# Attention inner loop: weighing in two halves of 256 queries, one ring of seven single PSUM banks, one exponential per head

## The chip, the cores and the metric

The kernel runs on one NeuronCore of a Trainium2 chip. It is written for five engines that each work through their own list of instructions in order: TensorE (PE in the profile, with its weight loads as PEld), VectorE (DVE), ScalarE (ACT), GpSimd (POOL) and SyncE (SP, which issues most DMAs). The metric is the device time of one execution, in microseconds (us); lower is better. All times below are of this one core.

## The reference

One transformer block over 2048 tokens with 576 features: pre-norm attention with 32 heads of 18 features, then a gated GELU network, both with a residual.

```python
# x: [1, 2048, 576]; H = 32, Dh = 18, Df = 4608
def _A_ref(x, wqkv, wo):
    qkv = (x @ wqkv).reshape(B, S, 3, H, Dh).transpose(2, 0, 3, 1, 4)
    q, k, v = qkv[0], qkv[1], qkv[2]
    scores = jnp.einsum("bhqd,bhkd->bhqk", q, k) * Dh ** -0.5
    o = jnp.einsum("bhqk,bhkd->bhqd", softmax(scores), v)
    return o.transpose(0, 2, 1, 3).reshape(B, S, D) @ wo

h  = x + _A_ref(layernorm(x), wqkv, wo)
h2 = h + einsum(gelu(layernorm(h) @ w_gate) * (layernorm(h) @ w_up), w_down)
```

## The kernel before

The program has three stages. The first normalizes the tokens, splits matrices into a high and a low half-precision part, and makes the queries, keys and values. The second is attention, and the change lies there. The third is the gated network.

**Blocks and steps.** The attention loop (L1219) runs over 32 blocks `n` (`NS`), each of one group of four heads and 512 queries. Inside a block it runs over 16 key tiles `kt` of 128 keys. One pass of that inner loop is called a step here, and an even step with the odd one behind it a pair of steps, since the pattern of the work repeats every two. A block is eight pairs.

**What a step does.**

- Scores. `scores_pair` (L667) is called twice. It multiplies 128 keys with 512 queries for two heads into the two halves of a double bank of PSUM (`pair`, two of them, used in turn): two matmuls (L674) of 56 rows each, one on array rows 0 to 55, the other on rows 64 to 119. One ACT instruction (L676) takes the exponential of both halves, 128x1024, into a buffer `pes` in the region `WK`. The double bank is free again when that exponential has ended.
- Maxima. A softmax needs the largest score of each query. `maxima` (L740) computes them a block and a half ahead of the scores. For each pair of steps it makes eight units of 128 queries by 512 keys, each a matmul (L621) of 54 rows into a single bank. Six of them are reduced by DVE to one maximum per query (L633). The other two go together: `over` is passed through a Relu by ACT (L627) into a row buffer, and `both` is added to that row and reduced by a custom DVE instruction (L631). `max_banks` (L611) issues one or two units in one go, and the loop takes five such portions per pair. The single banks are three, used in turn (`m_ring`, the first three of `singles`). At the end of a block's units `max_finish` (L638) reduces the maxima over the keys (L642) and sends them through POOL and two DMAs into the query rows.
- Weighing. `weigh` (L678) multiplies the exponentials of the step before with the values, for four heads, into the accumulator, the fourth of the single banks. Each head has 32 columns of the array (18 values, a one whose sum is the divisor, and padding). The operands are single precision, and the program's four matmuls of 512 queries are eight matmul records in the trace, which run as two batches of four at a time.

When a block's last weighing is done, in the first step of the next block, `out_block` (L688) starts: ACT copies the accumulator into `oT` (L694), a DMA fetches the sums, at `kt` 2 POOL inverts them (a power of -1 over 128x16, L703, and one correction), and at `kt` 4 the result is scaled and written into the transposed input of the output projection.

**What sets the order.** In this stage PE, DVE, ACT and POOL carry out their instructions in the order in which the program text issues them (a manual schedule); semaphores are the only waits. So the order of the calls inside the loop is the order on each engine. An even step before is: a portion of maxima, scores of heads 0 and 1, a portion, scores of heads 2 and 3, other work, a portion, the weighing of the step before. An odd step leaves out the middle portion. The other work (`fill`, `side`) is empty in most blocks; in the last three blocks it holds the output projection of finished queries (`wo_block`) and preparations for the third stage.

Before the loop, the maxima of a block and a half are made beside the remaining products for queries, keys and values (L1216).

Of the kernel before, what the change touches and what calls it, by code (L numbers as in the profile page):

```python
# [12 lines left out]
F32 = mybir.dt.float32  # L13
# [5 lines left out]
P = 128  # L19
# [12 lines left out]
def tile_block(  # L32
# [43 lines left out]
    psp = pairs_in.enter_context(tc.tile_pool(name="psp", bufs=1, space=bass.MemoryType.PSUM))  # L76
    pairs2 = [psp.tile([P, 2, 512], F32, name=f"pair{i}") for i in range(2)]

# [3 lines left out]

    pair_ring = ring(pairs2)
    m_ring = ring(singles)
# [274 lines left out]
    def v_rows(t):  # L359
        for i in range(2):  # L360
            pt = next(pair_ring)[:, 0]
# [61 lines left out]
    def idle_products(n):  # L423

        for _ in range(n):
            nc.tensor.matmul(pairs2[0][:, 0], id16, parts[0][:, :512], start=True, stop=True)

    def turned(t0):

        cols = slice(t0 * P, (t0 + 2) * P)  # L430
        pts = [pairs2[0][:, 1], pairs2[1][:, 0], next(m_ring), next(m_ring)]
# [12 lines left out]
        nc.scalar.copy(XT[:, NK, cols], pt[:, : 2 * P])  # L444
# [165 lines left out]

    def max_banks(n, mx, todo):  # L611

        g, qc = divmod(n, NB)
        pms = []
        for kind, t, kc, h in todo:
            Q, K = sets[g % 2][h // 2]
            q0 = qc * TB + t * P
            r = half(h % 2, R1)
            pm = next(m_ring)
            keys = steps[g % 2][r, kc // 2] if kind == "over" else K[r, kc * TB : (kc + 1) * TB]  # L620
            nc.tensor.matmul(pm[:, :TB], Q[r, q0 : q0 + P], keys, start=True, stop=True)  # L621
            pms.append(pm)
        for (kind, t, kc, h), pm in zip(todo, pms):
            dst = mx[:, t, h, kc : kc + 1]
            if kind == "over":
                row = next(rows_of)
                nc.scalar.activation(row, pm[:, :TB], AF.Relu)  # L627
                excess.append(row)
            elif kind == "both":
                row = excess.pop(0)  # L630
                nc.vector.tensor_tensor_reduce(row, pm[:, :TB], row, 1.0, LOWEST, ALU.add, ALU.max, dst)  # L631
            else:
                nc.vector.tensor_reduce(dst, pm[:, :TB], axis=AX.X, op=ALU.max)  # L633

# [31 lines left out]

    def scores_pair(n, kt, pr):  # L667

        g, qc = divmod(n, NB)
        pS = next(pair_ring)  # L670
        Q, K = sets[g % 2][pr]
        for j in range(2):
            r = half(j, R1 + 2)
            nc.tensor.matmul(pS[:, j, :TB], K[r, kt * P : (kt + 1) * P],  # L674
                             Q[r, qc * TB : (qc + 1) * TB], start=True, stop=True)
        nc.scalar.activation(pes[(2 * kt + pr) % NPE], pS[:, :, :TB], AF.Exp, scale=ex_reg)  # L676

    def weigh(n, kt, acc):  # L678
        for hh in range(4):
            nc.tensor.matmul(acc[32 * hh : 32 * hh + 32, :TB],  # L680
                             Vg[n // NB][:, kt * G4 + hh * VC : kt * G4 + hh * VC + 32],
                             pes[(2 * kt + hh // 2) % NPE][:, hh % 2],
                             start=(kt == 0), stop=(kt == NT - 1))

# [3 lines left out]
    def out_block(n, acc):  # L688
# [4 lines left out]
        oT = oTs[n % 2]  # L693
        nc.scalar.copy(oT, acc[:, :TB])  # L694
        R = 4 * TB // P
# [4 lines left out]
        if n < NS - NB:  # L700
            den, rc = rc, small.tile([P, R], F32, tag="rp", name="rp")
            re = small.tile([P, R], F32, tag="re", name="re")
            nc.gpsimd.tensor_tensor(rc, den, minus_one.to_broadcast([P, R]), op=ALU.pow)  # L703
            nc.gpsimd.tensor_mul(re, den, rc)
# [37 lines left out]
    def maxima():  # L742

        for n in range(NS):
# [449 lines left out]
    def other_products():  # L1194
        for b in range(1, NB):
            yield from v_block(b)
        for j in (1, 6, 2, 7, 3, 8):
            for b in range(1, NB):
                yield from qk_tile(j, b, next(pair_ring)[:, 0])

# [15 lines left out]
    for i in range(5 * AHEAD // 4):  # L1216
        take(mxs, 2)
# [53 lines left out]
    run(side)  # L1271
    weigh(*prev)
    ob = out_block(prev[0], prev[2])
# [102 lines left out]
```

## Time and profile before

| | us |
|---|---|
| median of 3 runs | 2652.98 (2652.97 to 2656.34) |
| the profiled execution | 2654.51 |
| its span in the trace | 2652.7 |
| attention loop in that span, first exponential to last | 216.6 to 1417.7 |

The span is the stretch from the first to the last instruction in the trace; the execution's time is 1.8 us longer. In the loop the granted clock of TensorE is 1.00. The whole profile is one execution. Its page gives busy time by engine and by source line; the timeline gives instructions in order of time, with neighbours of one kind merged (x2 is two of them, and the time is from the first one's start to the last one's end). An engine starts its next instruction before the one before has ended, so the distance from start to start is less than the duration. A PE record shows when a matmul was dispatched; two matmuls on different rows of the array run at the same time.

Busy shares in two stretches, from the windows view:

```profile
1284.80:1332.80 48.00, 46.35 (x333) 16.18 (x325) 42.03 (x90) 34.94 (x42) 32.01 (x43) 1.00 0.15 38
1381.20:1417.70 36.50, 33.27 (x242) 9.36 (x239) 29.23 (x64) 31.76 (x35) 28.55 (x43) 1.00 0.66 97
```

The columns are the stretch, its length, the busy time (and number of instructions) of PE, PEld, DVE, ACT and POOL, the granted clock, the share of the DMA engines that is busy and the GB/s that they move. The first is block 29, with projection products beside the attention; the second is block 31, the last, in which no maxima are left to make.

### The profile page before, as it was taken

To read this page: it belongs to the slowest core of one execution; us is meant where nothing else is said; L and a number is where in the kernel's file an instruction comes from. 1 tells how busy PE (TensorE), PEld (TensorE's weight loads), DVE (VectorE), ACT (ScalarE), POOL (GpSimd) and SP (SyncE) were. 2 spreads that over 40 slices of the span, in tenths; PEclk is the share of its full clock that TensorE was granted. 3 is DMA by queue.
4 is the path that set the end of the run, shared out by engine and by line. 5 is a ranking of instruction groups with operands and counts; after the bars stand their busy time and mean duration, and the time that the engine had idled before them with its cause. 6 is when DMAs were issued, how large, how long until landed. Compare 5 with 4: busy or idle time off the path is not lost.

```text
span 2652.7 us, 44543 instructions
## 1 busy us (share of the span) xinstructions
PE 2585.1 (97%) x16669; PEld 1118.4 (42%) x16669; DVE 2012.4 (76%) x3856; ACT 1621.0 (61%) x2128; POOL 788.2 (30%) x1076
## 2 busy tenths in 40 slices
PE   7999999999999999999999999999999999999999
PEld 4542222222222222222234555555555555555555
DVE  7368999999999999999967766666666666666653
ACT  5227999999999999999865433333333333333332
POOL 4200442221323232322666432222222222222221
PEclk9999999999999999999999999999999999999999
DMA  7411210010101010100116311010101010111110
GB/s 215 97 49 39 56 42 18 27 31 19 43 15 41 15 43 19 40 17 19 39 51 130 73 42 38 25 38 27 36 27 36 27 36 28 35 29 34 30 58 36
DMA packets 169099, 114.11 MB, mean 43 GB/s; under 512 B 88504, under 2 KB 147404, under 8 KB 168882
## 3 DMA queue, kind: packets, MB, share of 16 engines
q1 hardware_dynamic: 161198, 98.47, 13.9%
q0 software_dynamic: 7552, 12.79, 1.9%
q8 instruction: 130, 2.13, 0.3%
q14 instruction: 87, 0.71, 0.1%
q10 hardware_dynamic: 132, 0.01, 0.0%
HBM read 76.51 MB, written 15.01 MB: 35 GB/s over the span
## 4 chain that ended last, share of the span: by engine, by line
PE 68%; ACT 16%; issue 8%; DVE 4%; DMA 2%; POOL 2%; SPq 1%; ACTq 0%; DVEq 0%; POOLq 0%
PE more L1097 14%; PE bank L1097 14%; PE bank L300 11%; ACT WK L676 11%; PE bank L680 9%; PE more L300 8%; PE bank L621 7%; ACT nat L627 4%; PE pair L300 4%; PE pair L674 2%; DVE mx L633 1%; DMA nat<-rc 1%; DVE st L188 0%; DMA V<-V 0%; ACT nat L694 0%
## 5 line engine op out<-in xcount | busy, mean ns | idle before, releaser
L676 ACT ACTIVATE WK<-pair 128x1024 f32<-128x1024 f32 x1024 | 1000.0, 1041 | 83.4 <-PE pair L674 83.1
L633 DVE TENSOR_REDUCE mx<-bank 128x1 f32<-128x512 f32 x1552 | 975.7, 683 | 44.3 <-PE bank L621 33.6
L680 PE MATMUL bank<-WK,V 128*32 128x512 f32 x4096 | 547.1, 605 | 0.2 <-ACT nat L694 0.2
L300 PEld LDWEIGHTS <-WK 128*128 128x128 f16 x3456 | 338.8, 98 | 91.8 <-ACT WK L1108 1.7
L1097 PEld LDWEIGHTS <-W 128*128 128x128 f16 x2394 | 234.0, 98 | 283.2 <-issue 5.5
L621 PE MATMUL bank<-W 54*128 54x512 f16 x896 | 258.1, 379 | 14.5 <-DVE mx L633 2.2
L621 PE MATMUL bank<-A 54*128 54x512 f16 x904 | 250.9, 380 | 19.2 <-DMA nat<-qk_hi 3.2
L703 POOL TENSOR_TENSOR rp<-rc,minus_one 128x16 f32<-128x16 f32 x28 | 81.9, 2927 | 540.2 <-DMA rc<-nat 540.2
L300 PE MATMUL more<-W,WK 128*128 128x288 f16 x1728 | 235.9, 286 | 2.2 <-ACT WK L1108 1.4
L300 PE MATMUL bank<-W,WK 128*128 128x288 f16 x1728 | 236.7, 287 | 0.0
L1097 PE MATMUL bank<-X,W 128*128 128x512 f16 x792 | 223.8, 379 | 0.0
L674 PE MATMUL pair<-W 56*128 56x512 f16 x1024 | 210.0, 380 | 4.1 <-ACT WK L676 3.1
L674 PE MATMUL pair<-A 56*128 56x512 f16 x1024 | 212.1, 380 | 0.5 <-DMA A<-mT 0.3
L1097 PE MATMUL bank<-V,W 128*128 128x512 f16 x720 | 202.4, 379 | 0.4 <-ACT tmp L1147 0.3
L968 POOL TENSOR_TENSOR A<-A 128x384 f32<-128x384 f32 x136 | 137.1, 1029 | 200.4 <-DMA A<-in_B_w_up_dram 101.3
L621 PEld LDWEIGHTS <-W 54*128 54x128 f16 x1024 | 75.1, 93 | 284.2 <-issue 266.3
L631 DVE CUSTOM_DVE_ANT_0 nat<-bank,nat 128x512 f32<-128x512 f32 x248 | 171.4, 691 | 25.4 <-PE pair L674 2.4
L621 PEld LDWEIGHTS <-A 54*128 54x128 f16 x1024 | 71.6, 93 | 272.1 <-issue 250.8
L1111 POOL TENSOR_TENSOR WK<-tmp,WK 128x512 f16<-128x512 f32 x73 | 87.9, 1203 | 308.4 <-ACT WK L1108 308.3
L1115 ACT COPY tmp<-more 128x512 f32<-128x512 f32 x36 | 21.0, 583 | 239.1 <-PE more L1097 198.9
L627 ACT ACTIVATE nat<-bank 128x512 f32<-128x512 f32 x248 | 151.5, 611 | 14.7 <-PE bank L621 14.7
L680 PEld LDWEIGHTS bank<-WK,V 128*32 128x32 f32 x4096 | 81.1, 108 | 178.2 <-issue 163.4
(312 smaller groups left out, 3270.8 us busy)
## 6 DMA issues: line engine op xcount, KB each, us to landing
A<-in_B_w_down_dram SPq DMA_DIRECT2D x8, 1152.0 KB
nat<-rc SPq DMA_DIRECT2D x32, 256.0 KB
A<-in_B_w_gate_dram SPq DMA_DIRECT2D x64, 128.0 KB
A<-in_B_w_up_dram SPq DMA_DIRECT2D x64, 128.0 KB
qk_hi<-tmp SPq DMA_DIRECT2D x36, 128.0 KB
qk_lo<-tmp SPq DMA_DIRECT2D x36, 128.0 KB
out_dram<-nat SPq DMA_DIRECT2D x16, 288.0 KB
X<-nat SPq DMA_DIRECT2D x100, 36.0 KB
```

The source lines that it names most:

```text
L300: nc.tensor.matmul(dst, a, b, start=(i == 0), stop=(i == len(pairs) - 1))
L621: nc.tensor.matmul(pm[:, :TB], Q[r, q0 : q0 + P], keys, start=True, stop=True)
L627: nc.scalar.activation(row, pm[:, :TB], AF.Relu)
L631: nc.vector.tensor_tensor_reduce(row, pm[:, :TB], row, 1.0, LOWEST, ALU.add, ALU.max, dst)
L633: nc.vector.tensor_reduce(dst, pm[:, :TB], axis=AX.X, op=ALU.max)
L674: nc.tensor.matmul(pS[:, j, :TB], K[r, kt * P : (kt + 1) * P], Q[r, qc * TB : (qc + 1) * TB], start=True, stop=True)
L676: nc.scalar.activation(pes[(2 * kt + pr) % NPE], pS[:, :, :TB], AF.Exp, scale=ex_reg)
L680: nc.tensor.matmul(acc[32 * hh : 32 * hh + 32, :TB], Vg[n // NB][:, kt * G4 + hh * VC : kt * G4 + hh * VC + 32], pes[(2 * kt + hh // 2) % ...
L703: nc.gpsimd.tensor_tensor(rc, den, minus_one.to_broadcast([P, R]), op=ALU.pow)
L968: op(W8[:, d], W8[:, a], W8[:, b])
L1097: nc.tensor.matmul(bank, w, x_, start=start and i == 0, stop=i == len(mm) - 1, skip_group_check=not start)
L1111: nc.gpsimd.tensor_sub(hl[:, 2 * i + j], v, hh[:, 2 * i + j])
```

## The change

In words:

- The two double banks become four single ones, and in the loop all seven banks beside the accumulator are one ring, `m_ring`, out of which scores and maxima take their banks one after the other as the program issues them.
- `scores_pair` becomes `score`: one head, one matmul, one exponential over 128x512.
- `max_banks` becomes `max_bank`: one unit at a time. The order of the eight units of a pair is slightly different.
- `weigh` is a generator of two halves of 256 queries. Each half has its own four matmuls.
- The order inside a step is written as a string: `s` one head's scores, `m` one unit of maxima, `w` one half of the weighing, `f` the other work. It is `ssmsmmfwmsw` in an even step and `mssmssmfwwm` in an odd one.
- The copy of the accumulator (L694) goes to DVE, except in the last two blocks.
- POOL's power of -1 over 128x16 becomes four over 128x4, and the later parts of `out_block` come at `kt` 3 and 5 in place of 2 and 4.
- In the first stage the products use the four new single banks in turn where they used the first half of each of two double banks.

```diff
-    pairs2 = [psp.tile([P, 2, 512], F32, name=f"pair{i}") for i in range(2)]
+    quads = [psp.tile([P, 512], F32, name=f"quad{i}") for i in range(4)]
...
-    def scores_pair(n, kt, pr):
+    def score(n, kt, hh):
 
         g, qc = divmod(n, NB)
-        pS = next(pair_ring)
-        Q, K = sets[g % 2][pr]
-        for j in range(2):
-            r = half(j, R1 + 2)
-            nc.tensor.matmul(pS[:, j, :TB], K[r, kt * P : (kt + 1) * P],
-                             Q[r, qc * TB : (qc + 1) * TB], start=True, stop=True)
-        nc.scalar.activation(pes[(2 * kt + pr) % NPE], pS[:, :, :TB], AF.Exp, scale=ex_reg)
+        pS = next(m_ring)
+        Q, K = sets[g % 2][hh // 2]
+        r = half(hh % 2, R1 + 2)
+        nc.tensor.matmul(pS[:, :TB], K[r, kt * P : (kt + 1) * P],
+                         Q[r, qc * TB : (qc + 1) * TB], start=True, stop=True)
+        nc.scalar.activation(pes[(2 * kt + hh // 2) % NPE][:, hh % 2], pS[:, :TB], AF.Exp, scale=ex_reg)
 
     def weigh(n, kt, acc):
-        for hh in range(4):
-            nc.tensor.matmul(acc[32 * hh : 32 * hh + 32, :TB],
-                             Vg[n // NB][:, kt * G4 + hh * VC : kt * G4 + hh * VC + 32],
-                             pes[(2 * kt + hh // 2) % NPE][:, hh % 2],
-                             start=(kt == 0), stop=(kt == NT - 1))
+        for q in range(2):
+            qs = slice(q * TB // 2, (q + 1) * TB // 2)
+            for hh in range(4):
+                nc.tensor.matmul(acc[32 * hh : 32 * hh + 32, qs],
+                                 Vg[n // NB][:, kt * G4 + hh * VC : kt * G4 + hh * VC + 32],
+                                 pes[(2 * kt + hh // 2) % NPE][:, hh % 2, qs],
+                                 start=(kt == 0 and q == 0), stop=(kt == NT - 1 and q == 1))
+            yield
...
-        nc.scalar.copy(oT, acc[:, :TB])
+        (nc.scalar.copy if n >= NS - 2 else nc.vector.tensor_copy)(oT, acc[:, :TB])
...
-            nc.gpsimd.tensor_tensor(rc, den, minus_one.to_broadcast([P, R]), op=ALU.pow)
+            for c in range(0, R, 4):
+                nc.gpsimd.tensor_tensor(rc[:, c : c + 4], den[:, c : c + 4],
+                                        minus_one.to_broadcast([P, 4]), op=ALU.pow)
...
-                for todo in (((over, t, k + 1, 0), ("one", t, k, 1)),
-                             (("one", t, k + 1, 1),),
-                             (("one", t, k, 2), ("one", t, k, 3)),
-                             ((both, t, k, 0),),
-                             (("one", t, k + 1, 2), ("one", t, k + 1, 3))):
-                    max_banks(n, mx, todo)
+                for unit in (("one", t, k, 1), (over, t, k + 1, 0), ("one", t, k + 1, 1), ("one", t, k, 2),
+                             ("one", t, k, 3), (both, t, k, 0), ("one", t, k + 1, 2), ("one", t, k + 1, 3)):
+                    max_bank(n, mx, *unit)
                     yield
...
-    m_ring = ring(singles[:3])
+    m_ring = ring(singles[:3] + quads)
+    STEPS = ("ssmsmmfwmsw", "mssmssmfwwm")
...
-            take(mxs)
-            scores_pair(n, kt, 0)
-            if kt % 2 == 0:
-                take(mxs)
-            scores_pair(n, kt, 1)
-            if n < NS - 1 or kt < 11:
-                take(fill, 2)
-            take(side)
-            take(mxs)
-            if prev is not None:
-                weigh(*prev)
-                if prev[0] != n:
-                    ob = out_block(prev[0], prev[2])
-                    next(ob)
+            heads = iter(range(4))
+            halves = weigh(*prev) if prev is not None else iter(())
+            for step_no, step in enumerate(STEPS[kt % 2]):
+                if step == "s":
+                    score(n, kt, next(heads))
+                elif step == "m":
+                    take(mxs)
+                elif step == "w":
+                    take(halves)
+                    if kt == 0 and step_no == OUT_AT and prev is not None:
+                        ob = out_block(prev[0], prev[2])
+                        next(ob)
+                else:
+                    if n < NS - 1 or kt < 11:
+                        take(fill, 2)
+                    take(side)
...
-            if n and kt in ((1 if n == NS - 1 else 3, 6) if late else (2, 4)):
+            if n and kt in ((1 if n == NS - 1 else 3, 6) if late else (3, 5)):
```

How this moves instructions on three engines:

On PE, around the weighing of one step in the middle of the loop, before (L621 maxima, L674 scores, L680 weighing, each matmul behind its weight load):

```order
L621 LDWEIGHTS A
L621 MATMUL bank_66<-A 128x512 [waits Activation_49]
L621 LDWEIGHTS A
L621 MATMUL bank_67<-A 128x512 [waits DVE_49]
L680 MATMUL bank_69<-WK,V 32x512 x4
L621 LDWEIGHTS A
L621 MATMUL bank_68<-A 128x512 [waits DVE_49]
```

And on PE in an even step now (L619 maxima, L669 scores, L677 weighing):

```order
L619 MATMUL quad_74<-A 128x512 [waits DVE_49]
L677 MATMUL bank_69<-WK,V 32x256 x4
L619 LDWEIGHTS A
L619 MATMUL quad_75<-A 128x512 [waits DVE_49]
L669 LDWEIGHTS A
L669 MATMUL quad_76<-A 128x512 [waits Activation_49]
L677 MATMUL bank_69<-WK,V 32x256 x4
```

One weighing of an even step has become two of half the width, with one unit of maxima and one head's scores between them; in an odd step the two halves stand together (`x8`).

On ACT, one pair of steps and the start of the next before (L627 Relu, L676 exponentials):

```order
L627 ACTIVATE nat<-bank_68 128x512 [waits PE_49]
L676 ACTIVATE WK<-pair_73 128x1024 [waits PE_49,Activation_49]
L676 ACTIVATE WK<-pair_74 128x1024 [waits PE_49,Activation_49]
L676 ACTIVATE WK<-pair_73 128x1024 [waits PE_49,Activation_49]
L676 ACTIVATE WK<-pair_74 128x1024 [waits PE_49,Activation_49]
L627 ACTIVATE nat<-bank_67 128x512 [waits PE_49]
```

And the same on ACT now (L623 Relu, L671 exponentials):

```order
L623 ACTIVATE nat<-bank_67 128x512 [waits DVE_49,PE_49]
L671 ACTIVATE WK<-quad_74 128x512 [waits PE_49]
L671 ACTIVATE WK<-quad_76 128x512 [waits PE_49,Activation_49]
L671 ACTIVATE WK<-bank_66 128x512 [waits PE_49]
L671 ACTIVATE WK<-bank_68 128x512 [waits PE_49,Activation_49]
L671 ACTIVATE WK<-quad_73 128x512 [waits PE_49,Activation_49]
L671 ACTIVATE WK<-quad_76 128x512 [waits PE_49]
L671 ACTIVATE WK<-bank_66 128x512 [waits PE_49]
L671 ACTIVATE WK<-bank_68 128x512 [waits PE_49]
L623 ACTIVATE nat<-quad_73 128x512 [waits DVE_49,PE_49]
```

Between two Relus stand eight exponentials of 512 columns where four of 1024 stood.

On DVE, where a block's sums leave the accumulator (L627 the custom instruction that was L631, L629 the maxima, L692 the copy), now:

```order
L629 TENSOR_REDUCE mx<-quad_76 128x1 [waits PE_49]
L629 TENSOR_REDUCE mx<-bank_66 128x1 [waits PE_49]
L692 COPY nat<-bank_69 128x512 [waits DMAHW7_49,PE_49]
L629 TENSOR_REDUCE mx<-bank_68 128x1 [waits PE_49]
L627 ISA nat,mx<-quad_75,nat 128x512 [waits PE_49]
L627 ISA mx 128x1
```

The copy is new on DVE, once in a block, behind the third maximum of an even step and ahead of the first one of the odd step; before, it stood on ACT between two exponentials.

More of the change, by code (lines that the diff above doesn't have):

```diff
@@ L81, in ring @@
             yield from items
-    pair_ring = ring(pairs2)
+    p_ring = ring(quads)
     m_ring = ring(singles)
@@ L360, in v_rows @@
         for i in range(2):
-            pt = next(pair_ring)[:, 0]
+            pt = next(p_ring)
             yield from accumulate(pt[:, :HALF], products(
@@ L425, in idle_products @@
         for _ in range(n):
-            nc.tensor.matmul(pairs2[0][:, 0], id16, parts[0][:, :512], start=True, stop=True)
+            nc.tensor.matmul(quads[0], id16, parts[0][:, :512], start=True, stop=True)
     def turned(t0):
         cols = slice(t0 * P, (t0 + 2) * P)
-        pts = [pairs2[0][:, 1], pairs2[1][:, 0], next(m_ring), next(m_ring)]
+        pts = [quads[1], quads[2], next(m_ring), next(m_ring)]
         for pt, c0 in zip(pts, (0, 2, NK + 1, NK + 3)):
@@ L609, in key_steps, with max_bank @@
                               k.rearrange("r h s i -> r h (s i)"))
-    def max_banks(n, mx, todo):
+    def max_bank(n, mx, kind, t, kc, h):
         g, qc = divmod(n, NB)
[L614 to L633, printed above, removed]
+        Q, K = sets[g % 2][h // 2]
+        q0 = qc * TB + t * P
+        r = half(h % 2, R1)
+        pm = next(m_ring)
+        keys = steps[g % 2][r, kc // 2] if kind == "over" else K[r, kc * TB : (kc + 1) * TB]
+        nc.tensor.matmul(pm[:, :TB], Q[r, q0 : q0 + P], keys, start=True, stop=True)
+        dst = mx[:, t, h, kc : kc + 1]
+        if kind == "over":
+            row = next(rows_of)
+            nc.scalar.activation(row, pm[:, :TB], AF.Relu)
+            excess.append(row)
+        elif kind == "both":
+            row = excess.pop(0)
+            nc.vector.tensor_tensor_reduce(row, pm[:, :TB], row, 1.0, LOWEST, ALU.add, ALU.max, dst)
+        else:
+            nc.vector.tensor_reduce(dst, pm[:, :TB], axis=AX.X, op=ALU.max)
     mms = [const.tile([P, P], F16, name=f"mm{i}") for i in range(2)]
@@ L1198, in other_products @@
             for b in range(1, NB):
-                yield from qk_tile(j, b, next(pair_ring)[:, 0])
+                yield from qk_tile(j, b, next(p_ring))
     second = split_matrix(1, 0, None, lambda: load_matrix(w_up, 1, nc.gpsimd), space=3, held=True)
@@ L1216, in tile_block @@
     for i in range(5 * AHEAD // 4):
-        take(mxs, 2)
+        take(mxs, 3 + (i % 5 == 4))
         take(fill, 2 + (i % 5 in (1, 3)))
-    m_ring = ring(singles[:3])
+    m_ring = ring(singles[:3] + quads)
+    STEPS = ("ssmsmmfwmsw", "mssmssmfwwm")
+    OUT_AT = STEPS[0].rindex("w")
     prev = None
@@ L1225, in tile_block @@
         for kt in range(NT):
[L1226 to L1239 removed]
+            heads = iter(range(4))
[10 more added lines that the diff above has]
+                        next(ob)
+                else:
+                    if n < NS - 1 or kt < 11:
+                        take(fill, 2)
+                    take(side)
             prev = (n, kt, acc)
[L1241 removed]
+            if n and kt in ((1 if n == NS - 1 else 3, 6) if late else (3, 5)):
                 take(ob)
@@ L1271, in tile_block @@
     run(side)
-    weigh(*prev)
+    run(weigh(*prev))
     ob = out_block(prev[0], prev[2])
```

## The prediction

> **What bounds the kernel now.** I read the page first, then the windows of single blocks, the timeline of one pair of steps, engine by engine, and last the chain of waits. From the page:
>
> ```profile
> span 2652.7 us, 44543 instructions
> PE 2585.1 (97%) x16669; PEld 1118.4 (42%) x16669; DVE 2012.4 (76%) x3856; ACT 1621.0 (61%) x2128; POOL 788.2 (30%) x1076
> L676 ACT ACTIVATE WK<-pair 128x1024 f32<-128x1024 f32 x1024 | 1000.0, 1041 | 83.4 <-PE pair L674 83.1
> L633 DVE TENSOR_REDUCE mx<-bank 128x1 f32<-128x512 f32 x1552 | 975.7, 683 | 44.3 <-PE bank L621 33.6
> L680 PE MATMUL bank<-WK,V 128*32 128x512 f32 x4096 | 547.1, 605 | 0.2 <-ACT nat L694 0.2
> ```
>
> The two costliest groups belong to ACT and DVE, and both lie in the loop. How long a block takes follows from an instruction that comes once in each, the copy of the sums (durations, then first and last start); the window below is one block:
>
> ```profile
> L694 ACT COPY nat<-bank x24: 586/629/630, 408.6 to 1250.0; 128x512 f32<-128x512 f32 x24
> 438.92:475.55 36.63, 35.84 (x256) 9.07 (x256) 35.24 (x67) 34.48 (x42) 7.34 (x11) 1.00 0.05 14
> ```
>
> (1250.0 - 408.6) / 23 = 36.58 us a block, or about 4.55 a pair of steps. PE, DVE and ACT are each busy for 34 to 36 of these, so shares don't tell which is the bound. Start-to-start distances do. PE over one pair:
>
> ```profile
> 803.40 0.39 PE L621 MATMUL bank<-nat,A 54*128 54x512 f16 x1
> 803.40 0.39 PE L621 MATMUL bank<-A 54*128 54x512 f16 x1
> 803.62 0.38 PE L674 MATMUL pair<-W 56*128 56x512 f16 x2
> 803.86 0.37 PE L621 MATMUL bank<-A 54*128 54x512 f16 x1
> 804.09 0.39 PE L674 MATMUL pair<-W 56*128 56x512 f16 x2
> 804.58 0.39 PE L621 MATMUL bank<-A 54*128 54x512 f16 x2
> 804.90 1.07 PE L680 MATMUL bank<-WK,V 128*32 128x512 f32 x8
> 805.90 0.39 PE L621 MATMUL bank<-A 54*128 54x512 f16 x1
> 805.91 0.90 PE L674 MATMUL pair<-W 56*128 56x512 f16 x4
> 806.63 0.40 PE L621 MATMUL bank<-A 54*128 54x512 f16 x2
> 806.95 1.07 PE L680 MATMUL bank<-WK,V 128*32 128x512 f32 x8
> 807.95 0.39 PE L621 MATMUL bank<-nat,A 54*128 54x512 f16 x1
> ```
>
> ACT and DVE:
>
> ```profile
> 802.10 1.94 ACT L676 ACTIVATE WK<-pair 128x1024 f32<-128x1024 f32 x2 [0.29 <-PE pair L674]
> 803.92 0.60 ACT L627 ACTIVATE nat<-bank 128x512 f32<-128x512 f32 x1
> 804.40 1.96 ACT L676 ACTIVATE WK<-pair 128x1024 f32<-128x1024 f32 x2
> 806.64 1.94 ACT L676 ACTIVATE WK<-pair 128x1024 f32<-128x1024 f32 x2 [0.28 <-PE pair L674]
> 808.47 0.60 ACT L627 ACTIVATE nat<-bank 128x512 f32<-128x512 f32 x1
> 825.91 0.68 DVE L633 TENSOR_REDUCE mx<-bank 128x1 f32<-128x512 f32 x1
> 826.69 0.22 DVE L642 TENSOR_REDUCE m<-mx 128x16 f32<-128x64 f32 x1
> 826.83 2.48 DVE L633 TENSOR_REDUCE mx<-bank 128x1 f32<-128x512 f32 x4
> 829.39 0.69 DVE L631 CUSTOM_DVE_ANT_0 nat<-bank,nat 128x512 f32<-128x512 f32 x1
> ```
>
> And the chain of waits through this pair:
>
> ```profile
> 804.04 0.50 ACT nat L627
> 804.54 0.04 issue
> 804.58 0.39 PE bank L621 x2
> 804.97 1.00 PE bank L680 x8
> 805.97 0.32 PE bank L621
> 806.29 0.27 PE pair L674 x2
> ...
> 806.64 0.23 ACT WK L676
> ...
> 807.56 1.02 ACT WK L676
> 808.58 0.50 ACT nat L627
> ```
>
> It is a loop: the Relu's end frees a single bank for PE (804.58); its last two maxima and a weighing follow, during which PE makes no score (804.90 to 805.90); then scores, on which ACT waits 0.28 (806.64); two exponentials; the next Relu at 808.47, 4.55 after the last. No engine is full; too few banks tie them together. With work always there, each would need for a pair:
>
> - ACT: an exponential every (1.94 - 1.04) = 0.90, a Relu 0.48 (803.92 to 804.40): 4 x 0.90 + 0.48 = 4.08.
> - DVE: a maximum every (2.48 - 0.68) / 3 = 0.60, and I count the custom one the same: 7 x 0.60 = 4.20. Its late start in the rows (829.39, 0.08 after 826.83 + 2.48) I take for its wait on a matmul behind the weighing.
> - PE: matmuls on different array rows share a place, and a place takes 0.22 (803.40 to 803.62). The first group has five places, the second four: seven distances of 0.22. From the last place to a weighing it is 0.31 (the second of the two at 804.58 is a little later), and a weighing keeps PE for 1.00. 7 x 0.22 + 2 x 0.31 + 2 x 1.00 = 4.16.
>
> **The change part by part.**
>
> *Weighing in halves (PE).* A weighing is two batches: 1.07 less one matmul's 0.605 leaves 0.465 from its first to its last matmul, of which some 0.02 is the spread of the four in a batch, so 0.45 from batch to batch; the remaining 1.00 - 0.45 = 0.55 is the second batch with 0.10 of emptying the array. Half as many columns should halve the streaming but not the emptying: an estimate of 0.24 from batch to batch and 0.33 behind the last. A half alone is 0.57, two halves together 3 x 0.24 + 0.33 = 1.05. The new order gives groups of four, one and four places between weighings (neighbours on opposite array rows share one): six distances of 0.22, three entries of 0.31, then 2 x 0.57 + 1.05. Sum 1.32 + 0.93 + 2.19 = **4.44**, 0.28 more than before: 0.19 of it is a third switch to weighing and back. The Trainium skill's page TensorEngine Tiling (Array Packing), section Key Properties, says that changing the tiling mode drains the engine; it speaks against the change, the trace agrees (0.31 in place of 0.22 on the way in, 0.10 on the way out), and a sum with the drain hidden would give 4.25. Bounds of the new switch: nothing to 0.19 for each of the four halves.
>
> *One exponential per head (ACT).* 512 columns aren't in the trace as an exponential. Bounds: half of 0.90, 0.45, to the Relu's whole duration, 0.61. I take the Relu's distance, 0.48, for the same shape from PSUM on the same engine. 9 x 0.48 = **4.32**, 0.24 more.
>
> *Seven banks (all three).* The stall in the loop above goes, and the next is late instead. I number the sixteen matmuls of a pair's scores and maxima from the first score of the even step; each needs the bank of the one seven before it. With op 16 (the last maximum, behind the double half) at 0, PE's places put ops 7 and 8 at 1.54, 9 at 2.41, 14 at 2.85, 15 at 3.07, the double half at 3.38, the next op 16 at 4.43. A waiting DVE starts 0.46 after a matmul (0.38, and 0.07 to 0.09 as between 806.55, where that chain's scores end, and 806.64). Ops 16, 3, 6 and 7 go through DVE at 0.60 each, so op 7 starts at 2.26 and its bank is free at 2.26 + 0.68 + 0.05 = 2.99. Op 14 takes it 0.14 late, but op 15 shares the following place, so nothing moves. Op 15 needs the bank of op 8, ACT's fifth instruction in this count: 0.52 + 4 x 0.48 + 0.66 = 3.10, 0.03 late. So PE sets the pair, at 4.44 to 4.46, and ACT and DVE fit beneath it by 0.1 to 0.25: narrow.
>
> *The copy on DVE.* Bounds 0.60 (a maximum) to 0.77 (with the 0.16 by which the custom instruction, which has two waits, starts after 826.83 + 4 x 0.60); I take 0.69 in duration. It waits for the second half of the even step, then stands behind op 7: 2.26 + 0.60 = 2.86, done at 3.55. Queued behind it are ops 9, 12, 15 and 16, and PE's next double half, which writes the same accumulator, waits until 3.60 where it wanted 3.38. With the 0.10 that DVE is then late for op 6 of the next pair this is **0.32 a block**. ACT loses the 0.47 of L694, which it doesn't miss.
>
> *max_finish (L642)* was on DVE before: 825.91 to 826.83 is 0.92 in place of 0.60. Now its 0.32 delays op 7, and so op 14, by 0.24 net: **0.24 a block**.
>
> *POOL and SP.* Four powers of 4 columns in place of one:
>
> ```profile
> L703 POOL TENSOR_TENSOR rp<-rc,minus_one 128x16 f32<-128x16 f32 x28 | 81.9, 2927 | 540.2 <-DMA rc<-nat 540.2
> ```
>
> Between 2.9 and 4 x 2.9 = 11.7 us in all; I take 3, since the elements are as many. POOL is busy 7.3 of 36.6 us in that window. Behind the powers stand the correction and, on POOL, the next `max_finish`, whose result is due half a block (18 us) later: that covers it, and if the cover were gone, scores at a block's start would wait. The later `kt` of `out_block`'s parts moves its DMAs on SP past at most the loads of the next group; their results aren't read before the projection. I cost both at nothing. So too the four banks of the first stage, where PE is full in the stretch with most products:
>
> ```profile
> 140.00:210.00 70.00, 70.00 (x362) 29.99 (x362) 44.32 (x74) 14.38 (x29) 0.72 (x4) 1.00 0.18 60
> ```
>
> *Sum.* A block 8 x 4.44 + 0.32 + 0.24 = 36.1 against 36.58: 0.5 less, in the 28 blocks without projection products, 14 us. The last three have products that fill PE, and as many mode switches as before, since `f` now touches `w`. But where no maxima are left ACT is the bound:
>
> ```profile
> 1396.75 6.67 ACT L676 ACTIVATE WK<-pair 128x1024 f32<-128x1024 f32 x7 [0.29 <-PE pair L674]
> ```
>
> (6.67 - 1.04) / 6 = 0.94 against 2 x 0.48, some 40 times: 1 us more. So -13 from the profiled execution's 2654.5. That one is 1.5 above the median of the runs; from the median, 2653.0 - 13 = **2640**.
>
> **The rivals.**
>
> 1. *Nothing gained.* Three engines that need 4.2 to 4.44 of 4.55 in a fixed order lose the remaining 0.1 to waits on each other, as happened before, when none needed over 4.20. For: op 15's margin is already spent. Against: seven banks are two whole units deeper. 2653.
> 2. *Slower, by the switches on PE.* If the two halves that stand together don't run on without a gap (weights loaded anew, the array emptied), each pair has a fourth exit and entry, 0.19: 4.63 a pair, 37.6 a block, 28 x 1.0 + 1 = 29 more, 2682. It decides from 4.50 a pair on ((36.58 - 0.56) / 8), only 0.06 above my sum. For: before, PE's weight loads don't start until a weighing has emptied. Against: within a weighing the second batch follows the first without that gap.
> 3. *Slower, by ACT.* Its bound passes 4.50 once an exponential takes over 0.50. At 0.52, a third of the way from the Relu's distance to its duration, a pair is 8 x 0.52 + 0.48 = 4.64, 37.7 a block, about 2684; at 0.61 over 2800. Against: the Relu row, and the step from 0.48 to 0.90 with twice the columns. The Trainium skill's page ScalarE: Activation LUTs, section What ACT_TABLE_LOAD costs, gives 186 ns + 0.833 ns per column, of which neighbours hide 93: that makes 0.52 for 512 columns, so by that page this rival would win; its 0.95 for 1024 stands against 0.90 here.
> 4. *Faster than I say.* If the third switch's 0.19 hides, PE falls to 4.25 or less, and DVE is the bound: 8 x 4.2 + 0.7 + 0.3 = 34.6 with ACT's 8 x 4.32 the same; 2 us a block, 2600. Against: the 0.31 and 0.10 recur at every weighing above.
>
> **How the numbers follow.** My case 0.47, with 2630 to 2651 of its own (0.05 a pair either way is 11 us); rival 1 0.20; rival 2 0.20; rival 3 0.05; rival 4 0.08. Over 0.2% (5 us), about what a measurement can tell from no change, counts: faster 0.52 (rival 4, nearly all of mine, a little of rival 1), same 0.21, slower 0.27. The range leaves out rival 4 and the worse ends of 2 and 3: 2615 to 2690.
>
> **What would show it.** Halves: PE from a lone weighing's first matmul to the next other matmul at 0.57, two together at 1.05. ACT: exponentials 0.48 apart where they queue. DVE: idle some 0.2 in each pair, with op 16 waiting for PE. The chain of waits should run mostly along PE, not through the Relu. The copies on DVE lie 36.1 apart. I am wrong if PE waits for banks in most pairs, or if a double half is longer than 1.1.

## The result, and the profile after

| | before | after |
|---|---|---|
| time, median of the runs (us) | 2653.7 (2652.97 to 2656.34) | 2636.14 (2633.43 to 2638.20) |
| profiled execution and its span (us) | 2654.5, 2652.7 | 2638.2, 2636.4 |
| one block, median distance of the same exponential in neighbouring blocks (us) | 36.55 | 35.83 |
| a pair of steps without the copy or `max_finish` (us) | 4.51 to 4.59 | 4.426 |
| blocks 29 to 31, from the last exponential before them to their own last, start to start (us) | 131.9 | 137.1 |

The kernel became faster by 0.7%: the ratio to before is 0.9931, 95% interval 0.9914 to 0.9949. The same kernel, run again later beside three of the experiments, gave 2632.76 and 0.9933 (0.9920 to 0.9947).

From the page of the kernel after (head, busy times, shares of the chain that ended last, two of the costliest groups):

```profile
span 2636.4 us, 53635 instructions
...
PE 2589.5 (98%) x20765; PEld 1200.4 (46%) x20765; DVE 2014.7 (76%) x3886; ACT 1662.0 (63%) x3122; POOL 819.3 (31%) x1160
...
PE 87%; DVE 6%; POOL 2%; DMA 2%; issue 1%; SPq 1%; ACT 1%; DVEq 0%; ACTq 0%; POOLq 0%
...
L671 ACT ACTIVATE WK<-quad 128x512 f32<-128x512 f32 x1169 | 655.4, 620 | 24.0 <-PE quad L669 18.4
...
L702 POOL TENSOR_TENSOR rp<-rc,minus_one 128x4 f32<-128x4 f32 x112 | 111.3, 1012 | 382.6 <-DMA rc<-nat 382.6
```

Busy times hardly differ from before; the shares of the chain do. It is now 87% PE and 1% ACT, where the page of before has

```profile
PE 68%; ACT 16%; issue 8%; DVE 4%; DMA 2%; POOL 2%; SPq 1%; ACTq 0%; DVEq 0%; POOLq 0%
```

In the loop alone (400 to 1250 us), the chain of before is 37% ACT (26.4% exponentials, 10.3% Relu), where ACT's exponentials are 0.2% of that of after.

The period of a block is again read from the copy of the sums, now on DVE (durations, first and last start):

```profile
L692 DVE COPY nat<-bank x24: 681/681/686, 404.9 to 1230.5; 128x512 f32<-128x512 f32 x24
```

(1230.5 - 404.9) / 23 = 35.90 us, 0.68 less than the 36.58 of before. One block as a window (its length, then busy time of PE, PEld, DVE, ACT and POOL):

```profile
437.94:473.78 35.84, 35.75 (x388) 11.54 (x384) 35.32 (x67) 35.72 (x74) 8.42 (x14) 1.00 0.05 14
```

PE is busy for all but 0.09 of 35.84. Its timeline over one pair of steps:

```profile
775.51 0.64 PE L677 MATMUL bank<-WK,V 128*32 128x256 f32 x8
776.09 0.39 PE L619 MATMUL bank<-A 54*128 54x512 f16 x1
776.09 0.39 PE L669 MATMUL bank<-W 56*128 56x512 f16 x1
776.41 0.64 PE L677 MATMUL bank<-WK,V 128*32 128x256 f32 x8
...
777.43 0.43 PE L669 MATMUL bank<-W 56*128 56x512 f16 x2
777.65 0.38 PE L619 MATMUL bank<-A 54*128 54x512 f16 x1
777.95 1.07 PE L677 MATMUL bank<-WK,V 128*32 128x256 f32 x16
778.96 0.39 PE L619 MATMUL quad<-A 54*128 54x512 f16 x1
...
779.62 0.39 PE L619 MATMUL bank<-A 54*128 54x512 f16 x1
779.94 0.42 PE L677 MATMUL bank<-WK,V 128*32 128x256 f32 x4
```

No row has an idle time in brackets. PE walks through its list in 4.43 (775.51 to 779.94): nine places, two lone halves (a half of the weighing with other matmuls before and behind it) and a double half (two halves in a row). A lone half takes 0.58 (775.51 to 776.09), an entry, from the last place to a weighing, 0.32 (776.09 to 776.41), the double half 1.01 (777.95 to 778.96). The chain of waits over the same pair, from the second lone half to the double half, has no piece of ACT or DVE:

```profile
776.48 0.57 PE bank L677 x8
777.05 0.32 PE quad L619
777.37 0.22 PE quad L669 x2
...
777.59 0.28 PE bank L669 x2
777.87 0.16 PE bank L619
778.02 1.00 PE bank L677 x16
```

ACT and DVE fit beneath it. ACT's busy time in the block, 35.72 of 35.84, counts durations, which overlap; where its instructions queue they start 0.48 apart, and nine of them need 4.3 of the 4.43. Two rows from ACT's timeline:

```profile
776.44 0.67 ACT L623 ACTIVATE nat<-quad 128x512 f32<-128x512 f32 x1
776.91 0.68 ACT L671 ACTIVATE WK<-bank 128x512 f32<-128x512 f32 x1
```

And from DVE's:

```profile
778.01 0.68 DVE L627 CUSTOM_DVE_ANT_0 nat<-quad,nat 128x512 f32<-128x512 f32 x1
...
778.62 0.69 DVE L629 TENSOR_REDUCE mx<-bank 128x1 f32<-128x512 f32 x1
779.38 0.69 DVE L629 TENSOR_REDUCE mx<-quad 128x1 f32<-128x512 f32 x1
```

The Relu's successor follows it at 0.47; at 778.62 the maximum follows the custom instruction at 0.61, and the next one, op 16 behind the double half, starts 0.16 later than a queued one would (779.38 in place of 779.22): DVE waits for PE there.

**Where the time went.** Blocks are told apart here by one mark: a block runs from the start of the last exponential of the block before to the start of its own last one. The marks that the section on the profile before and the expectations below call first exponentials are these same ones: the 216.6 there is the start of a table load on ACT, and the first exponential starts at 217.9, so each mark counted from the load lies one exponential early.

In the two profiled executions the span of after is 16.3 us shorter. Blocks 1 to 27 give 19.0 (0.70 each). Blocks 29 to 31 lose 5.2, and 4.5 in the second profiled execution of after. Block 28 loses 1.1, but with this order it takes 37.51 to 39.31 from run to run, so that loss isn't shown to be the change's. What stands ahead of block 1, block 0 included, is 0.1 shorter, and what stands behind the start of the last exponential 3.5. That last part takes 1231.6 to 1234.0 in all other executions of this study, whatever the kernel, and 1236.0 in the one of before, so I don't count it as the change's. The loss at the end is seen in two windows of after: block 29, and the last block up to the end of its last exponential.

```profile
1266.80:1315.74 48.94, 45.45 (x450) 18.63 (x446) 42.91 (x92) 36.43 (x73) 32.43 (x45) 1.00 0.15 38
1366.24:1404.54 38.30, 38.09 (x376) 13.44 (x373) 30.14 (x65) 33.51 (x67) 27.40 (x40) 1.00 0.64 107
```

Before, the first of these lasted 48.00 and the second 36.50 with PE busy for 33.27 of it (windows above, in the section on the profile before). In the last block, which has no maxima, PE is now busy to 99%, and the chain of waits there is PE's but for 2%:

```profile
by line: PE bank L677 59.3%; PE quad L669 15.4%; PE bank L669 12.3%; PE quad L300 6.1%; PE bank L300 4.8%; ACT nat L692 1.6%; PE quad L138 0.7%; issue 0.2%; ACTq L692 0.1%
```

### The profile page after: what moved, and what is told of

Same layout as the page of the kernel before. It is cut to its first block, busy times and chain, and to the rows that moved or that the text cites. A ratio compares the mean times of both kernels' runs of the same rounds, so it can differ in the third digit from the quotient of the medians.

```text
span 2636.4 us, 53635 instructions
## 1 busy us (share of the span) xinstructions
PE 2589.5 (98%) x20765; PEld 1200.4 (46%) x20765; DVE 2014.7 (76%) x3886; ACT 1662.0 (63%) x3122; POOL 819.3 (31%) x1160
## 4 chain that ended last, share of the span: by engine, by line
PE 87%; DVE 6%; POOL 2%; DMA 2%; issue 1%; SPq 1%; ACT 1%; DVEq 0%; ACTq 0%; POOLq 0%
PE bank L677 18%; PE more L1094 14%; PE bank L1094 14%; PE bank L300 9%; PE more L300 8%; PE quad L619 7%; PE bank L619 6%; PE quad L300 4%; PE quad L669 4%; DVE mx L629 3%; PE bank L669 3%; DVE nat L692 1%; ACT WK L671 0%; DMA A<-qk_lo 0%; POOL A L249 0%
## 5 line engine op out<-in xcount | busy, mean ns | idle before, releaser
L671 ACT ACTIVATE WK<-quad 128x512 f32<-128x512 f32 x1169 | 655.4, 620 | 24.0 <-PE quad L669 18.4
L677 PE MATMUL bank<-WK,V 128*32 128x256 f32 x8192 | 608.3, 389 | 2.4 <-DVE nat L692 0.4
L629 DVE TENSOR_REDUCE mx<-quad 128x1 f32<-128x512 f32 x834 | 552.6, 684 | 13.0 <-PE quad L669 3.0
L671 ACT ACTIVATE WK<-bank 128x512 f32<-128x512 f32 x879 | 504.8, 621 | 19.6 <-PE bank L669 17.6
L629 DVE TENSOR_REDUCE mx<-bank 128x1 f32<-128x512 f32 x718 | 478.6, 684 | 40.5 <-PE bank L619 33.0
L677 PEld LDWEIGHTS bank<-WK,V 128*32 128x32 f32 x8192 | 190.3, 108 | 270.8 <-issue 204.4
L702 POOL TENSOR_TENSOR rp<-rc,minus_one 128x4 f32<-128x4 f32 x112 | 111.3, 1012 | 382.6 <-DMA rc<-nat 382.6
L619 PE MATMUL quad<-W 54*128 54x512 f16 x510 | 190.5, 383 | 0.9 <-ACT WK L671 0.6
L619 PEld LDWEIGHTS <-W 54*128 54x128 f16 x1024 | 74.8, 94 | 244.3 <-issue 228.0
L619 PEld LDWEIGHTS <-A 54*128 54x128 f16 x1024 | 71.4, 94 | 233.9 <-issue 213.7
L619 PE MATMUL quad<-A 54*128 54x512 f16 x463 | 172.3, 384 | 0.6 <-ACT WK L671 0.6
L669 PE MATMUL quad<-A 56*128 56x512 f16 x585 | 171.5, 382 | 1.0 <-DMA A<-mT 0.6
L669 PE MATMUL quad<-W 56*128 56x512 f16 x584 | 169.6, 381 | 2.0 <-DVE mx L629 1.9
```

What stands on the lines that cost most here:

```text
L669: nc.tensor.matmul(pS[:, :TB], K[r, kt * P : (kt + 1) * P], Q[r, qc * TB : (qc + 1) * TB], start=True, stop=True)
L671: nc.scalar.activation(pes[(2 * kt + hh // 2) % NPE][:, hh % 2], pS[:, :TB], AF.Exp, scale=ex_reg)
L677: nc.tensor.matmul(acc[32 * hh : 32 * hh + 32, qs], Vg[n // NB][:, kt * G4 + hh * VC : kt * G4 + hh * VC + 32], pes[(2 * kt + hh // 2) % N ...
L702: nc.gpsimd.tensor_tensor(rc[:, c : c + 4], den[:, c : c + 4], minus_one.to_broadcast([P, 4]), op=ALU.pow)
```

## The experiments

The theory: before was held by the loop through the Relu and three single banks; after is held by PE's list of places and switches, and the order and the ring of seven are what let PE walk it. The rivals to tell apart: that single exponentials alone are the gain, that halves are only a cost, that the ring's size does nothing, and that the copy's new engine or POOL's powers matter. All ratios are to before, run on the same chip beside them; periods of a block are medians as in the table above, in the profiled execution.

**The weighing whole again**, at the place of its last half; all else as after.

```diff
     def weigh(n, kt, acc):
-        for q in range(2):
-            qs = slice(q * TB // 2, (q + 1) * TB // 2)
-            for hh in range(4):
...
+        for hh in range(4):
...
-    STEPS = ("ssmsmmfwmsw", "mssmssmfwwm")
+    STEPS = ("ssmsmmfmsw", "mssmssmfwm")
```

> The changed kernel with the weighing in one piece of 512 queries again, in both steps at the place of the last half; all else as changed. Three theories. PE count alone: a switch to weighing and back goes from each pair, 0.2 us; ACT's 4.3 us a pair is then the bound, a block takes about 34.8 us and the kernel 2608. Ring and order: PE has less to do, but a loop through ACT takes over (four exponentials from op 1 to op 8 at 0.48, the bank of op 8 freed after 0.66, the entry 0.31, the weighing 1.00, a score's 0.52 until its exponential starts): 4.40 us a pair against 4.43, a block about 35.6 us, 2630 us. Halves matter (ACT starves behind a whole weighing, as before): 4.55 a pair or more, 2665 us or more.

Measured: 2641.99 us, ratio 0.9966 (0.9952 to 0.9980); a plain pair 4.463, a block 36.18. The timeline of PE and, behind it, the chain of waits over the same place:

```profile
810.61 0.39 PE L619 MATMUL bank<-A 54*128 54x512 f16 x1
...
811.28 0.87 PE L619 MATMUL bank<-A 54*128 54x512 f16 x2
...
812.10 1.07 PE L675 MATMUL bank<-WK,V 128*32 128x512 f32 x8
```

```profile
810.67 0.32 PE bank L619
...
811.04 0.69 DVE mx L629
811.73 0.04 issue
811.77 0.37 PE bank L619
```

PE lost a switch and got a wait. Op 7 needs the bank of op 16; that matmul starts at 810.61, its reduction at 811.04, and the bank is free at 811.77, 1.16 later, where op 7's place among the others would be 0.88 later (four places of 0.22): 0.28 of waiting, about what the switch had cost. In the kernel after, the first half of the even step stands between the two and covers it. So the halves are worth 0.35 us a block here (36.18 to 35.83), not by being halves but by the work they put in front of op 7. That this wait, not ACT, would bind without them I had not foreseen. A whole weighing at the place of the first half, which would also stand in front of op 7 and save the switch, was not run, so it stays open whether the cut itself is needed.

**Two rings**: scores take the four quads, maxima the three singles, in the new order.

```diff
-        pS = next(m_ring)
+        pS = next(s_ring)
...
-    m_ring = ring(singles[:3] + quads)
+    m_ring = ring(singles[:3])
+    s_ring = ring(quads)
```

> The changed kernel with two rings: scores take the four new single banks in turn, maxima the three old ones. Theory that the shared ring is what took the stall away: with three banks, the second maximum of the even step (op 6) waits for DVE to finish op 16, 1.20 us after op 16's matmul in place of 0.66, so a pair takes 4.9 us, a block about 40 us, the kernel 2740 to 2750. Rival, that the halves or the single exponentials made the gain and the ring only holds it: 2636, no change.

Measured: 2744.34 us, ratio 1.0352 (1.0334 to 1.0369); a plain pair 4.91, a block 39.49. PE waits for a single bank (the idle time and its releaser in brackets):

```profile
806.75 0.37 PE L619 MATMUL bank<-A 54*128 54x512 f16 x1 [0.35 <-DVE mx L629]
807.05 0.64 PE L677 MATMUL bank<-WK,V 128*32 128x256 f32 x8
```

The banks are the same seven; that scores and maxima share them in the order of the program is worth 0.48 a pair in this order.

**The old order**, with ring, single exponentials, halves (both together) and copy as after.

```diff
-    STEPS = ("ssmsmmfwmsw", "mssmssmfwwm")
+    STEPS = ("mmssmssfmmww", "mssssfmmww")
```

> The changed kernel with the order of before: two maxima, two scores, one maximum, two scores, two maxima and the whole weighing in an even step; one maximum, four scores, two maxima and the weighing in an odd one (the halves stand together, so they act as one). Seven banks in one ring and single exponentials stay. Theory that seven banks need the new order too: the last score of the even step holds the bank that the last score of the odd one waits for, and behind that stand two maxima and a weighing; the loop is 0.66 + 0.22 + 0.31 + 1.00 + 0.52 + 4 x 0.48 = 4.62 a pair, a block about 37.4 us, 2680 us. Rival, that banks alone made the gain: 2636 or, with one switch less on PE, down to 2608.

Measured: 2670.39 us, ratio 1.0077 (1.0060 to 1.0094); pairs 4.55 to 4.67, a block 37.14. The chain of waits runs through ACT and DVE again:

```profile
802.87 0.99 ACT WK L671 x2
...
803.90 0.37 PE quad L619
...
804.77 1.00 PE bank L677 x16
...
807.95 0.37 PE bank L619 x2
808.31 2.47 DVE mx L629 x4
```

Two things follow. All parts of the change but its order make the kernel slower. And a weighing cut in halves that stay together costs PE what a whole one did (1.00, x16, as 1.00, x8, before).

**All four halves apart**: a fourth switch in each pair.

```diff
-    STEPS = ("ssmsmmfwmsw", "mssmssmfwwm")
+    STEPS = ("ssmsmmfwmsw", "mssmssfwmwm")
```

> The changed kernel with the two halves of the odd step also apart (one maximum between them). If PE is now the bound, its count goes up by the fourth switch less the places that are shared otherwise: 5 x 0.22 + 4 x 0.31 + 4 x 0.57 = 4.62 against 4.40 by the same count, 0.22 to 0.24 a pair, 1.8 us a block, 2686 us. If waits between ACT, DVE and PE are the bound and not PE's count, shorter holes on PE can only help: 2636 or a little less.

Measured: 2710.72 us, ratio 1.0227 (1.0210 to 1.0244); a plain pair 4.725, a block 38.41. PE's weighings, and the last scores ahead of one:

```profile
805.84 0.64 PE L677 MATMUL bank<-WK,V 128*32 128x256 f32 x8
...
807.38 0.64 PE L677 MATMUL bank<-WK,V 128*32 128x256 f32 x8
...
809.30 0.45 PE L669 MATMUL quad<-W 56*128 56x512 f16 x2
809.68 0.64 PE L677 MATMUL bank<-WK,V 128*32 128x256 f32 x8
...
810.57 0.64 PE L677 MATMUL bank<-WK,V 128*32 128x256 f32 x8
```

810.57 - 805.84 = 4.73. By the terms of the prediction it is five distances of 0.22, four entries of 0.31 and four lone halves of 0.57: 4.62. Most of the rest is one entry of 0.38, from the last place at 809.30 to 809.68: the second matmul of that place starts 0.07 late (0.45 for the two, 0.38 for one). The fourth switch, that late matmul included, costs 0.30 a pair (4.725 - 4.426), where rival 2 put 0.19, and the copy's pair grows to 5.02 and that of `max_finish` to 5.05. So a further switch costs at least what rival 2 put for it; that two halves which stand together bring one, as rival 2 had it, is not what the runs show (1.00 for the double half).

**The copy on ACT again**, as before the change.

```diff
-        (nc.scalar.copy if n >= NS - 2 else nc.vector.tensor_copy)(oT, acc[:, :TB])
+        nc.scalar.copy(oT, acc[:, :TB])
```

> The changed kernel with the accumulator's copy on ACT in all blocks. On DVE it costs 0.26 us a block in the trace (4.685 for its pair of steps in place of 4.426). Theory: ACT has 0.13 us to spare in a pair and the copy takes 0.47 there, so it delays the bank that PE needs for the next weighing by as much or more; 0.3 us a block, no change within 3 us. Rival, that ACT hides it: 7 us less. Rival, that ACT is as good as full: 0.5 us a block, 6 us more.

Measured: 2640.86 us, ratio 0.9962 (0.9948 to 0.9976), 8 us more than the kernel after beside it; a block 36.05. The first two pairs of a block last 4.77 and 4.56 where they lasted 4.43 and 4.68 with the copy on DVE: 0.22 a block, and 28 blocks make 6 of the 8 us. The theory, no change within 3 us, missed; the rival that ACT is as good as full, 6 us more, came nearer. On the page DVE has the greater share of busy time, but that is an average over all stages: in the block's window above ACT has 35.72 and DVE 35.32.

**One power for all 16 columns** on POOL, with the parts of `out_block` as early as before.

```diff
-            for c in range(0, R, 4):
-                nc.gpsimd.tensor_tensor(rc[:, c : c + 4], den[:, c : c + 4],
-                                        minus_one.to_broadcast([P, 4]), op=ALU.pow)
+            nc.gpsimd.tensor_tensor(rc, den, minus_one.to_broadcast([P, R]), op=ALU.pow)
...
-            if n and kt in ((1 if n == NS - 1 else 3, 6) if late else (3, 5)):
+            if n and kt in ((1 if n == NS - 1 else 3, 6) if late else (2, 4)):
```

> The changed kernel with one power of -1 over 128x16 on POOL again, and the later parts of the output block at steps 2 and 4. Theory: POOL has cover, no change within 2 us. Rival, that POOL's long instruction holds up DVE or the maxima behind it: 3 us or more slower.

Measured: 2635.03 us, ratio 0.9945 (0.9932 to 0.9959), within the spread of the kernel after (2630.62 to 2637.26 beside it); a block 35.83 as there. Powers and times of the parts do nothing that can be measured.

**The old order in the late blocks only.**

```diff
+    LATE = ("mmssmssfmmww", "mssssfmmww")
...
-            for step_no, step in enumerate(STEPS[kt % 2]):
+            steps_now = (LATE if late else STEPS)[kt % 2]
+            for step_no, step in enumerate(steps_now):
```

> The changed kernel, but the last three blocks, where projection products fill PE and the maxima run out, in the order of before with whole weighings (halves together). Those three take 137.1 us from their first to their last exponential in the changed kernel, 131.9 in the one before, 132.6 with the old order throughout. Theory that the halves' switches and their place cost what was lost there: 4.5 us less, 2631.5. Rival, that single exponentials and the shared ring cost it: no change.

Measured: 2632.09 us, ratio 0.9928 (0.9915 to 0.9942). In the trace, blocks 29 to 31 last 133.3 in place of 136.5 for the kernel after beside it, 3.2 of the 4.5 that were lost. The last block falls from 37.69 to 35.72, as short as before the change (35.50), block 30 from 49.87 to 48.78, block 29 hardly (48.90 to 48.78, and 48.01 before). What is block 29's hangs on the mark: from its own first exponential to that of block 30 it takes 52.74, 52.08 and 51.52. The last block as a window, up to the end of its last exponential:

```profile
1361.04:1397.71 36.67, 36.46 (x375) 13.82 (x373) 29.08 (x64) 32.67 (x67) 28.28 (x42) 1.00 0.63 104
```

PE is busy to 99% there too. The time differs from the kernel after by 0.7 us, which can't be told from none. So most of the late loss in the trace is the new order; whether its third switch or its places cost it was not tried apart, and no version better than the kernel after is shown.

**Before, with two exponentials of 512 columns** for each one of 1024; nothing else.

```diff
-        nc.scalar.activation(pes[(2 * kt + pr) % NPE], pS[:, :, :TB], AF.Exp, scale=ex_reg)
+        for j in range(2):
+            nc.scalar.activation(pes[(2 * kt + pr) % NPE][:, j], pS[:, j, :TB], AF.Exp, scale=ex_reg)
```

> The kernel before with one part of the change alone: each exponential of 128x1024 becomes two of 128x512, still from double banks and in the old order. Theory that before ran on a loop through ACT (two exponentials, the Relu, two maxima, a weighing, scores): the loop's two exponentials, 0.90 and 0.92, become four at 0.48, 0.09 more a pair, 0.7 us a block, 20 us in all, 1.0075 of the kernel before. Rival, that ACT's idle time of 0.4 us a pair hides it: no change.

Measured: 2685.52 us, ratio 1.0131 (1.0114 to 1.0148); a block 37.69, so 1.14 more where 0.7 was expected. The chain is the loop of before, longer:

```profile
802.47 0.50 ACT nat L627
...
803.01 0.39 PE bank L621 x2
803.40 1.00 PE bank L681 x8
...
805.54 1.57 ACT WK L677 x3
807.11 0.50 ACT nat L627
```

The next Relu follows the last by 4.64 here (802.47 to 807.11), where it was 4.55: exponentials stand in the loop, two of 512 columns take 0.05 more than one of 1024 (2 x 0.477 against 0.90), and over the block 0.14 a pair (1.14 / 8) of the 0.2 that four of these make comes through. By themselves single exponentials are a cost; it is the ring of single banks, which they allow, and the order that pay it back.

## Why the prediction was right

Its time was 4 us above the median, its range held it, and the mechanism is the one that it named. Step by step:

- **The bound before.** The loop through the Relu was read rightly. The chain of before had 16% ACT and 8% issue, that of after 1% and 1%; lengthening ACT's part of the loop alone lengthened each block by 1.1 us (two exponentials of 512), and dividing the banks again brought back a wait in every pair (two rings).
- **PE's list, 4.44 a pair.** Measured 4.426. A lone half is 0.57 as forecast; the double half is 1.00, not 1.05. Its first batch-to-batch distance is 0.24 and the time behind its last batch 0.33, as estimated, but the second and third distances are 0.215 (batches at 777.954, 778.194, 778.410 and 778.625, the next matmul at 778.958). The third switch doesn't hide: each switch shows 0.32 in place of 0.22 on the way in, and a fourth one adds 0.23 to 0.30, without and with the late matmul beside it. The Trainium skill's TensorEngine Tiling (Array Packing), section Key Properties, says that a change of tiling mode drains the engine; the trace agrees (0.32 in place of 0.22), and the page states no price. Rival 4, in which it hides, and rival 2, in which the halves together don't run on, fall by these rows.
- **ACT, 0.48 an exponential.** Measured 0.477 where they queue, the distance of the Relu, so rival 3 falls. By the Trainium skill's ScalarE: Activation LUTs, section What ACT_TABLE_LOAD costs (186 ns + 0.833 ns a column, with 93 ns overlapped by neighbours), it would be 0.52, as an estimate; the trace disagrees (0.477), and the measured distance decides.
- **Seven banks.** PE waits for none in the plain pair, so rival 1 falls; the two banks that the prediction found late cost nothing. It had op 14 late by 0.14 without effect; in the trace that matmul starts 0.06 behind the one that shares its place (777.43, 0.43 for the two and 0.37 for one), and op 15, which it had late by 0.03, follows in its place at 777.65. That this holds because a half of the weighing stands in front of op 7 came out only when it was taken away.
- **The custom instruction** as short as a maximum, its late start before a wait for PE: 0.61 to the next in the rows of after.
- **The copy, 0.32, and `max_finish`, 0.24 a block.** Their pairs are 4.685 and 4.593 against 4.426: 0.26 and 0.17. The durations were right (0.68 for the copy); what comes through to PE is 0.06 to 0.07 less in each. With 8 x 4.426 a block is 35.84, against 36.1 forecast.
- **POOL.** Four powers of 4 columns take 4 x 1.01 = 4.05 us, not 3; they stay covered, as the run with one power shows.
- **The late blocks, +1.** The step "as many mode switches as before, since `f` now touches `w`", with 1 us for ACT's exponentials, was mis-sized: they lose 5.2 in this execution and 4.5 in the other. In the last block PE, busy to 99%, is the bound, not ACT as I had it; with the old order there it is nearly back at its old length (35.72, 35.50 before). What the loss of block 29 is stays open.

So two mis-sizings of opposite sign nearly cancel: blocks 1 to 28 gain 17.9 where 14 was forecast, and the last three lose 5.2 where 1 was put. That leaves 12.7 for the loop against the 13 of the sum, and that it comes so near is luck. The rest of the 17.6 us between the medians lies outside these blocks or in the spread of the runs; no run shows which.

## What to carry to other kernels

When three engines are each busy nearly all the time and none is the bound, look for the loop of buffers between them: one ring used in the order of the program, with the work ordered so that the unit seven back is done when its bank is wanted, was worth 4% against the same banks in two rings (1.0352 / 0.9931). Price a kernel on an in-order engine by counting its places and its switches, since that count is what remains when the waits go. Cutting a long block of work into pieces paid here because a piece covers a wait; try the order with it, without which the same parts lost 0.8%.

## What the runs showed of the hardware that was not expected

- A bank that a maximum has filled comes back to PE 1.16 us after that matmul's start even with DVE idle: 0.43 to the reduction's start, 0.69 for it, 0.04 to the next matmul (the chain of the whole weighing). The prediction had these pieces (0.46, 0.68, 0.05); what was not expected is that they, and not an engine's share, bind where a whole weighing leaves op 7 too near to op 16.
- POOL's power does not go by its columns alone: 1.01 us for 128x4 and 2.93 for 128x16, four times the columns for 2.9 times the time.
- Cutting a weighing costs PE nothing while its halves stay together: four batches in a row take 1.00 (x16) as two of twice the columns did (x8), where 1.05 was forecast. One half by itself takes 0.57, more than half of that.
